# Twelve frequency groups: the second of two products replaced by ScalarE copies that exchange partition halves

## The chip, the cores and the metric

The kernel runs on one core of a Trainium2 chip. The metric is the time of one execution on the device in microseconds (us). The engines are PE (TensorE, matrix products into PSUM), DVE (VectorE), ACT (ScalarE), POOL (GpSimd, which works on SBUF only here) and SP (which issues DMAs); PEld is the loading of weights into PE.

## The reference

An input x of 2048 rows and 640 columns goes through two mixers, and a gate per row blends them:

```python
def _A_ref(x, wqkv, wo):       # 32 heads of 20, a window of 8 keys, every second row back
    qkv = (x @ wqkv).reshape(B, S, 3, H, Dh) ...
    logits = jnp.einsum("bhsd,bhswd->bhsw", q, kg) * scale
    attn = _softmax(where(mask, logits, -1e9))
    return einsum("bhsw,bhswd->bhsd", attn, vg).reshape(B, S, D) @ wo

def _B_ref(x, w_r, w_i):
    X = jnp.fft.rfft2(x)
    return jnp.fft.irfft2(X * (w_r + 1j * w_i), s=(S, D))

g = _sigmoid((x * gate_w).sum(-1, keepdims=True))
return g * a + (1 - g) * b
```

## The kernel before

Rows are held as 128 partitions of 16 rows j. The work has these stages. **qkv**: products of x and wqkv, split into two halves of precision, for even rows (`xe`) and odd rows (`xo`), written to a buffer in DRAM. **fold** and **cols**: the sums and differences of x that the spectrum needs, on DVE, and the first transform (tiles `fe`, `fx`, `z`). **attend**: per pair of head groups the products of q and k (`pr`, from a copy of q in a PSUM bank named `qbank`), their sums (`L`), maximum and exponential, the products with v on POOL (`pv`) and their sums on DVE (`o`); names such as `o4b6` carry the group, the half and the row. **freq**: the spectrum in 16 groups of frequencies, described below. **spatial** (tiles `oa`, `ob`, `ha`, `hb`, `h`, `y`): the transform back, odd rows first. **project**: the product with wo for even rows (`woa`, `wob`, `ya`), and at the very end for odd rows.

A frequency group g of `freq` works as follows. PE computes v and u out of zc, and DVE their sum and difference `ab`. PE multiplies `ab` with a table `tb`: `xa` and `xc` are the products of sum and difference, `xb` and `xd` the same with the table's columns in the turned order, which is the spectrum times the imaginary unit: the same numbers with their two halves of 64 partitions exchanged and one half negated. ACT copies `xa` and `xb` into `X`; POOL multiplies X by the weights `wp` and adds (`P`). DVE multiplies `xc` by a weight into `p` and `xd` by another in place, subtracts (`xd<-p,xd`), and adds to and subtracts from P (`s`). PE transforms `s` back (`g`), and ACT copies it into `zg`. The four products take their PSUM banks in turn out of two, BX = banks 3 and 4.

The order of all instructions is not written by hand. A planner records every operation with a duration and a delay (`Plan.cost`), sorts it by a list schedule forward and backward, then tries `AGAIN` random shifts of the priorities and keeps the best (`Plan.order`). Each engine runs its instructions in that order. Waits between engines come from a layer below, which sees the tiles that an instruction reads and writes. All instructions are issued from one line, L636 before and L638 after.

Of the kernel before, what the change touches and what calls it, by code (L numbers as in the profile page):

```python
# [27 lines left out]
BV, BU, BX, BG, BO = (0,), (1, 2), (3, 4), (5,), (6,)  # L28
# [127 lines left out]
class Plan:  # L156
# [84 lines left out]
    def cost(self, op, out, ins, k):  # L241
        n = max(int(np.prod(v.shape[1:])) for v in [out] + ins[:1])
        if op.name == "dma_start":
            op.busy, op.lat = {"SP": 0.45, "ACT": 0.45, "POOL": 1.0}[op.eng], LAND
            op.size = int(np.prod(out.shape)) * 4
            op.early = not hasattr(ins[0].tensor, "tag")
        elif op.eng == "PE":
            n = int(np.prod(out.shape[1:]))
            if op.name == "transpose":
                op.busy = 0.109  # L250
            elif ins[-1].dtype == F32R:
                op.busy = n / 2400 + 0.018
            else:
                op.busy = 4 * n / 2400 + 0.006
            op.lat = 0.25
        elif op.eng == "DVE":
            op.busy, op.lat = 0.075 + n / 960, 0.12
            two = sum(v.tensor.tag[:4] not in ("bank", "qban") for v in ins) == 2
            if op.name == "scalar_tensor_tensor":
                op.busy += 0.06  # L260
            elif op.name == "reciprocal":
                op.busy += n * 0.007
            elif two:
                op.two = True
        elif op.eng == "ACT":
            strided = any(len(v.ap) > 2 and v.ap[-1][0] > 1 for v in [out] + ins)
            op.busy, op.lat = 0.12 + n * (1.75e-3 if strided else 0.78e-3), 0.15
            if len(ins) > 1:
                op.busy += 0.1
        else:  # L270
            spread = any(v.ap[-1][0] == 0 for v in ins)
            op.busy, op.lat = 0.09 + n * (2e-3 if spread else 2.25e-3), 0.14
        if op.eng in ("DVE", "ACT", "POOL") and not op.size:
            op.busy *= PACE
# [192 lines left out]
                exec(*op.call)  # L467


TURNS, AGAIN, MOVE, SEED = 6, 60, 2.0, 2  # L470
DRAWS, SOONEST, LATER_BY = 3, 2.4, 0.6
ENGS = ("PE", "DVE", "ACT", "POOL", "SP")
RATE = 380e3
# [29 lines left out]
class Mixer:  # L503
# [64 lines left out]
    def work(self):  # L568
# [48 lines left out]
        p.chain = ""  # L617
        freq = [self.freq(g) for g in GORD]
        staged(freq, 4)
        p.chain = "even"  # L620
        for j in range(0, NJ, 2):
# [120 lines left out]
    def attend(self, par, h, step=4):  # L742
# [18 lines left out]
        for jj in range(0, 8, 2):  # L761
# [5 lines left out]
            else:  # L767
# [7 lines left out]
                in_=pr.rearrange("p j r (h d) -> p j r h d", d=HD),  # L775
                axis=AX.X,
                op=ALU.add,
# [3 lines left out]
        m = self.mr.next(f"m{nm}", 8, 4)  # L781
        V.tensor_reduce(out=m, in_=L, axis=AX.X, op=ALU.max)
        G.tensor_sub(L, L, m.unsqueeze(3).broadcast_to([128, 8, 4, 8]))
        A.activation(out=L, in_=L, func=AF.Exp, scale=SCALE)
        s = self.sr.next(f"s{nm}", 8, 4)
        V.tensor_reduce(out=s, in_=L, axis=AX.X, op=ALU.add)
        V.reciprocal(s, s)
        G.tensor_mul(L, L, s.unsqueeze(3).broadcast_to([128, 8, 4, 8]))
        yield
        for jj in range(0, 8, 2):  # L790
# [4 lines left out]
            for i in range(2):  # L795
# [4 lines left out]
                )  # L800
            V.tensor_reduce(out=o[:, jj % step : jj % step + 2], in_=pv, axis=AX.X, op=ALU.add)
            if jj % step == step - 2:
# [65 lines left out]
    def freq(self, g):  # L868

        p, ins = self.p, self.ins  # L870
        V, A, G, T, S = p.dve, p.act, p.pool, p.pe, p.sp
        zg, bt = self.zg, self.bt
        if g == 0:
            tb = self.one("tbfirst", 1280, tag="x7")
            S.dma_start(tb, ins["t_first"])
        else:
            if g % 3 == 1:
                self.mm = self.mdr.next(f"mm{g}", 3, 320)
                S.dma_start(self.mm, ins["t_mm"][(g - 1) // 3])
            tb = self.mm[:, (g - 1) % 3]  # L880
        wp = self.wpr.next(f"wp{g}", 4, 321)
        self.queue("wp").dma_start(wp, ins["ws"][g])

        zc = self.zcr.next(f"zc{g}", 6, NJ, 8)
        A.copy(zc[:, 0:3], zg[:, 0:3, :, 8 * g : 8 * g + 8])
        A.mul(zc[:, 3:6, :, 0:4], zg[:, 2:5, :, 8 * g + 4 : 8 * g + 8], -1.0)
        A.copy(zc[:, 3:6, :, 4:8], zg[:, 2:5, :, 8 * g : 8 * g + 4])

        def row(o, t, r, start, stop):
            T.matmul(o, zc[:, t].rearrange("p j c -> p (j c)"), r, start=start, stop=stop, skip_group_check=True)  # L890

        v = self.ps(BV, f"v{g}")[:, 0:321]
        row(v, 4, bt[:, 803:1124], True, False)
        row(v[:, 0:161], 3, bt[:, 642:803], False, False)
        row(v[:, 161:321], 5, bt[:, 1124:1284], False, True)
        vv = self.vsr.next(f"vs{g}", 321)
        A.copy(vv, v)
        u = self.ps(BU, f"u{g}")[:, 0:321]
        row(u, 1, bt[:, 161:482], True, False)
        row(u[:, 0:161], 0, bt[:, 0:161], False, False)  # L900
        row(u[:, 161:321], 2, bt[:, 482:642], False, True)

        ab = self.abr.next(f"ab{g}", 2, 321)
        V.tensor_add(ab[:, 0], u, vv)
        V.tensor_sub(ab[:, 1], u, vv)
        yield

        def col(nm, i, turned):

            o = self.ps(BX, f"{nm}{g}")[:, 0:321]  # L910
            if g == 0:
                c = 256 * i + 128 * turned
                T.matmul(o, tb[:, c : c + 128], ab[:, 0], start=True, stop=False)
                T.matmul(o, tb[:, 512 + c : 640 + c], ab[:, 1], start=False, stop=True)
            else:
                c = 0 if turned else 64
                T.matmul(o, tb[:, c : c + 128], ab[:, i], start=True, stop=True)
            return o

        X = self.Xr.next(f"X{g}", 2, 321)  # L920
        for i, nm in enumerate(("xa", "xb")):
            A.copy(X[:, i], col(nm, 0, i))
        P = self.Pr.next(f"P{g}", 2, 321)
        G.tensor_mul(P, X, wp[:, 0:2])
        G.tensor_add(P[:, 0], P[:, 0], P[:, 1])
        yield
        z, sz = col("xc", 1, 0), col("xd", 1, 1)
        t = self.p1r.next(f"p{g}", 321)
        V.tensor_mul(t, z, wp[:, 2])
        V.tensor_mul(sz, sz, wp[:, 3])  # L930
        V.tensor_sub(sz, t, sz)
        s = self.s12r.next(f"s{g}", 768)
        d0 = 321
        if g == 0:
            d0 = 449
            G.memset(s[:, 384:449], 0.0)
        V.tensor_add(s[:, 0:321], P[:, 0], sz)
        V.tensor_sub(s[:, d0 : d0 + 319], P[:, 0, 2:], sz[:, 2:])
        yield

        last = s[:, 640:768] if g == 0 else s[:, 512:640]
        chunks = [[(s[:, 0:128], 0)], [(s[:, 128:256], 0)], [(s[:, 256:384], 0)], [(s[:, 384:512], 1)], [(last, 1)]]
        if g == 0:
            chunks[2:4] = [[(s[:, 384:512], 1), (s[:, 256:321], 0)], [(s[:, 512:640], 1)]]
        for t0, n in ((0, 3), (3, 2)):
            o = self.ps(BG, f"g{g}_{t0}")
            for i in range(n):
                for w, back in chunks[t0 + i]:
                    m = tb[:, 1024 + 128 * back : 1152 + 128 * back] if g == 0 else tb[:, 192:320]
                    T.matmul(  # L950
                        o[0 : w.shape[1], i * 128 : i * 128 + 128],
                        w,
                        m,
                        start=(i == 0),
                        stop=(i == n - 1),
                        skip_group_check=True,
                    )
            A.copy(
                zg[:, t0 : t0 + n, :, 8 * g : 8 * g + 8],
                o[:, 0 : n * 128].rearrange("p (t j c) -> p t j c", t=n, c=8),  # L960
            )
# [166 lines left out]
POOL_PR = {u: (6,) for u in ((0, 3), (0, 4), (0, 5), (0, 7), (1, 0), (1, 1), (1, 3), (1, 4), (1, 5), (1, 7))}  # L1128


def build(tc, ins, out):
    Mixer(tc, ins, out).run()

# [43 lines left out]
```

## Time and profile before

| | us |
|---|---|
| median of 3 runs | 467.83 |
| lowest and highest | 467.37, 468.66 |
| span of the profiled execution | 465.3 |
| outside the span, median less span | 2.5 |

The page gives no time of the profiled execution beside its span, so the last row takes the median for it. The frequency stage lies from about 235 to 353 us, with attention beside it; spatial and the even projections follow to about 423, and the odd projections end the span. In the profile's rows a group is "line engine operation out<-in by names (numbers left out), shapes, count | busy us, mean ns | idle before us, and what ended it". A float32 product appears as two records, a product of the split type (fp32r) as one.

### The profile page before, as it was taken

To read this page: it belongs to the slowest core of one execution; us is meant where nothing else is said; L and a number is where in the kernel's file an instruction comes from. 1 tells how busy PE (TensorE), PEld (TensorE's weight loads), DVE (VectorE), ACT (ScalarE), POOL (GpSimd) and SP (SyncE) were. 2 spreads that over 40 slices of the span, in tenths; PEclk is the share of its full clock that TensorE was granted. 3 is DMA by queue.
4 is the path that set the end of the run, shared out by engine and by line. 5 is a ranking of instruction groups with operands and counts; after the bars stand their busy time and mean duration, and the time that the engine had idled before them with its cause. 6 is when DMAs were issued, how large, how long until landed. Compare 5 with 4: busy or idle time off the path is not lost.

```text
span 465.3 us, 7240 instructions
## 1 busy us (share of the span) xinstructions
PE 457.0 (98%) x2497; PEld 399.5 (86%) x2497; DVE 423.4 (91%) x555; ACT 205.2 (44%) x539; POOL 323.9 (70%) x264
## 2 busy tenths in 40 slices
PE   7999999999999999999999999999999999999997
PEld 4788888888889888899887788898888999988996
DVE  4699959999999999998999999999999997989784
ACT  5523346533335453257356465545444564333110
POOL 1003847999999879988698996767877997952300
PEclk9999999999999999999999999999999999999999
DMA  8999998796877968959998466567543321447732
GB/s 310 403 376 308 393 381 314 230 299 197 242 216 252 322 187 275 282 167 276 343 258 307 135 217 220 185 183 234 182 129 120 103 80 56 136 141 220 227 113 85
DMA packets 71700, 105.90 MB, mean 228 GB/s; under 512 B 20704, under 2 KB 50400, under 8 KB 71664
## 3 DMA queue, kind: packets, MB, share of 16 engines
q1 hardware_dynamic: 40624, 69.90, 46.0%
q10 hardware_dynamic: 30128, 31.55, 20.9%
q0 software_dynamic: 912, 4.00, 2.1%
q8 instruction: 19, 0.31, 0.3%
q14 instruction: 17, 0.14, 0.1%
HBM read 72.59 MB, written 32.84 MB: 227 GB/s over the span
## 4 chain that ended last, share of the span: by engine, by line
PE 82%; DVE 10%; DMA 4%; issue 2%; ACT 0%; ACTq 0%; DVEq 0%
PE qkv L636 43%; PE wob L636 6%; PE woa L636 6%; PE z L636 4%; PE ob L636 4%; PE oa L636 4%; PE u L636 2%; PE v L636 2%; PE hb L636 2%; PE g L636 2%; PE ha L636 2%; DVE xd L636 2%; DMA fx<-in_x 2%; PE oTp L636 2%; DVE s L636 1%
## 5 line engine op out<-in xcount | busy, mean ns | idle before, releaser
L636 PE MATMUL qkv<-w,xo 128*128 128x480 f32 (+1 forms) x480 | 110.7, 384 | 0.0
L636 PE MATMUL qkv<-w,xe 128*128 128x480 f32 (+1 forms) x465 | 104.1, 382 | 1.1 <-DVE xe L636 0.7
L636 PEld LDWEIGHTS qkv<-w,xe 128*128 128x128 f32 x465 | 87.3, 188 | 17.1 <-ACT xe L636 1.8
L636 PEld LDWEIGHTS qkv<-w,xo 128*128 128x128 f32 x480 | 89.8, 189 | 13.7
L636 ACT COPY ev<-qkv 128x480 f32<-128x480 f32 x64 | 35.4, 558 | 71.9 <-PE qkv L636 60.9
L636 PE MATMUL woa<-wo,oT 128*128 128x320 f32 x240 | 51.2, 317 | 0.1
L636 PE MATMUL wob<-wo,oT 128*128 128x320 f32 x240 | 50.4, 314 | 0.0
L636 PEld LDWEIGHTS wob<-wo,oT 128*128 128x128 f32 x240 | 39.0, 188 | 0.8 <-ACT ya L636 0.2
L636 PEld LDWEIGHTS woa<-wo,oT 128*128 128x128 f32 x240 | 39.0, 188 | 0.7 <-ACT oT L636 0.4
L636 POOL TENSOR_TENSOR w<-raw,w 128x480 fp32r<-128x480 f32 (+1 forms) x20 | 28.6, 1442 | 11.1 <-ACT w L636 11.1
L636 POOL TENSOR_TENSOR P<-X,wp 128x642 f32<-128x642 f32 x16 | 25.0, 1562 | 15.4 <-ACT X L636 15.4
L636 POOL DMA_DIRECT2D fd<-fx x6 | 4.3, 717 | 37.5 <-DMA raw<-in_wqkv 31.3
L636 POOL TENSOR_TENSOR yi<-yi,y 128x640 f32<-128x640 f32 x8 | 12.4, 1558 | 20.5 <-DMA yi<-ad 14.9
L636 ACT CAST oT<-oTp 128x384 fp32r<-128x384 f32 (+1 forms) x32 | 13.1, 427 | 29.9 <-PE oTp L636 25.2
L636 PEld LDWEIGHTS g<-mm,s 128*128 128x128 f32 x150 | 21.5, 191 | 3.6 <-ACT zg L636 0.2
L636 PE MATMUL g<-mm,s 128*128 128x128 f32 x150 | 22.7, 274 | 0.0
L636 PE MATMUL oa<-gt,zg 128*128 128x161 f32 (+1 forms) x96 | 22.1, 344 | 0.0
L636 PE MATMUL u<-bt,zc 128*128 128x321 f32 (+2 forms) x96 | 22.1, 344 | 0.0
L636 PE MATMUL v<-bt,zc 128*128 128x321 f32 (+2 forms) x96 | 22.1, 344 | 0.0
L636 PE MATMUL ob<-gt,zg 128*128 128x161 f32 (+1 forms) x96 | 21.0, 344 | 0.0
L636 ACT CAST w<-raw 128x480 fp32r<-128x480 f32 (+1 forms) x30 | 17.4, 594 | 7.4 <-DMA raw<-in_wqkv 2.2
L636 PEld LDWEIGHTS v<-bt,zc 128*128 128x128 f32 x96 | 16.3, 190 | 4.0 <-ACT vs L636 0.2
(301 smaller groups left out, 1118.7 us busy)
## 6 DMA issues: line engine op xcount, KB each, us to landing
qkvd<-ev ACTq DMA_DIRECT2D x32, 480.0 KB, 4.8
wp<-in_ws SPq DMA_DIRECT2D x16, 642.0 KB, 4.4
raw<-in_wqkv SPq DMA_DIRECT2D x25, 240.0 KB, 5.8
fx<-in_x SPq DMA_DIRECT2D x8, 641.0 KB, 9.0
ot<-od SPq DMA_DIRECT2D x16, 320.0 KB, 3.4
fd<-fx POOLq DMA_DIRECT2D x6, 640.0 KB, 8.5
f<-fd SPq DMA_DIRECT2D x6, 640.0 KB, 5.5
xt<-in_xT SPq DMA_DIRECT2D x8, 320.0 KB, 6.3
```

The costliest lines, as they stand in the source:

```text
L636: p.dve.memset(w, 0.0)
```

## The change

For the groups 4 to 15 the products `xb` and `xd` are gone. A helper `turn` makes the same values by two ACT operations over 64 partitions each: the lower half from the upper, negated, and the upper half from the lower. For X the source is `xa`, the target `X[:, 1]` in SBUF; for `xd` the source is `xc`, the target a PSUM bank taken from the same two. Such a group now takes three turns of the banks, not four. The planner gets 0.08 us more for an ACT operation with an operand that begins at partition 64 or above, and tries 100 shifts in place of 60. Groups 0 to 3 stay as they were.

```diff
@@ Plan.cost
             if len(ins) > 1:
                 op.busy += 0.1
+            if any(v.offset >= 64 * v.ap[0][0] for v in [out] + ins):
+                op.busy += 0.08
@@
-TURNS, AGAIN, MOVE, SEED = 6, 60, 2.0, 2
+TURNS, AGAIN, MOVE, SEED = 6, 100, 2.0, 2
@@ Mixer.freq
+        def turn(to, o):
+
+            A.mul(to[0:64], o[64:128], -1.0)
+            A.copy(to[64:128], o[0:64])
+
         X = self.Xr.next(f"X{g}", 2, 321)
-        for i, nm in enumerate(("xa", "xb")):
-            A.copy(X[:, i], col(nm, 0, i))
+        o = col("xa", 0, 0)
+        A.copy(X[:, 0], o)
+        if g in TURN:
+            turn(X[:, 1], o)
+        else:
+            A.copy(X[:, 1], col("xb", 0, 1))
...
-        z, sz = col("xc", 1, 0), col("xd", 1, 1)
+        z = col("xc", 1, 0)
+        if g in TURN:
+            sz = self.ps(BX, f"xd{g}")[:, 0:321]
+            turn(sz, z)
+        else:
+            sz = col("xd", 1, 1)
@@
+TURN = tuple(range(4, 16))
```

PE has 1979 products in the program in place of 2003, ACT 36 operations more; DVE, POOL and SP have the same instructions in another order. Three places of that order follow.

The first is DVE in group 8 of the frequency stage, before the change, from `ab` of group 9 on. What an instruction waits for stands in brackets, by engine or DMA queue.

```order
L636 TENSOR_TENSOR ab9_743<-u9_742,vs9_741 128x321 [waits PE_49]
L636 TENSOR_TENSOR ab9_743<-u9_742,vs9_741 128x321
L636 TENSOR_TENSOR p8_748<-xc8_746,wp8_722 128x321 [waits DMAHW5_49,PE_49]
L636 TENSOR_TENSOR pr5a4_536<-kt5a_530,qbank_63 128x1280 [waits Activation_49]
L636 TENSOR_TENSOR xd8_747<-xd8_747,wp8_722 128x321 [waits PE_49]
L636 TENSOR_TENSOR xd8_747<-p8_748,xd8_747 128x321 [waits DVE_49]
L636 TENSOR_TENSOR s8_749<-P8_737,xd8_747 128x321 [waits DVE_49,Pool_49]
```

The same place of DVE after the change:

```order
L638 TENSOR_TENSOR oT2_856<-oTp3_858,oT2_856 128x256 [waits Activation_49]
L638 TENSOR_TENSOR p8_743<-xc8_741,wp8_718 128x321 [waits DMAHW1_49,Activation_49]
L638 TENSOR_TENSOR pr5a4_536<-kt5a_530,qbank_63 128x1280
L638 TENSOR_TENSOR xd8_742<-xd8_742,wp8_718 128x321 [waits Activation_49]
L638 TENSOR_TENSOR xd8_742<-p8_743,xd8_742 128x321 [waits DVE_49]
L638 TENSOR_TENSOR s8_744<-P8_732,xd8_742 128x321 [waits DVE_49,Pool_49]
```

DVE's product p and its multiplication of xd waited for PE, and now for ACT (Activation). ACT's side of it in the changed order:

```order
L638 ACTIVATE X8_730<-xa8_731 64x321 [waits PE_49,Pool_49]
L638 COPY zg_210<-g6_3_725 128x32x8 [waits PE_49]
L638 COPY X8_730<-xa8_731 64x321
L638 CAST oT2_856<-oTp3_858 128x256 [waits PE_49]
L638 COPY X8_730<-xa8_731 128x321
L638 ACTIVATE xd8_742<-xc8_741 64x321 [waits PE_49,Activation_49]
L638 COPY xd8_742<-xc8_741 64x321 [waits DVE_49]
L638 COPY zg_210<-g7_0_739 128x48x8 [waits PE_49]
```

The second half copy waits for DVE (its p), so in this group ACT and DVE alternate. So it is in groups 4, 6, 7, 8, 9, 10 and 12; in 5, 11, 13 and 15 both half copies stand ahead of p, and in 14 p stands ahead of both.

The second place is ACT near 52 to 63 us, in the first attention group, before the change, from the last cast of the weight block w2 on:

```order
L636 CAST w2_4_159<-raw2_4_158 128x480
L636 COPY ev1_6_148<-qkv1_6_147 128x6x80
L636 CAST w3_0_173<-raw3_0_172 128x480
L636 CAST w3_1_175<-raw3_1_174 128x480
L636 CAST w3_2_177<-raw3_2_176 128x480
L636 COPY qbank_63<-q0a_340 128x160
L636 COPY L0a_341<-low_80 1x8x2
L636 COPY ev1_6_148<-qkv1_7_149 128x6x80
L636 COPY qbank_63<-q0b_356 128x160
```

And after the change:

```order
L638 CAST w2_4_159<-raw2_4_158 128x480
L638 DMA qkvd_64<-ev1_4_145 128x6x160
L638 COPY qbank_63<-q0a_340 128x160
L638 CAST w3_0_173<-raw3_0_172 128x480
L638 COPY qbank_63<-q0b_356 128x160
L638 CAST w3_1_175<-raw3_1_174 128x480
L638 COPY L0a_341<-low_80 1x8x2
L638 CAST w3_2_177<-raw3_2_176 128x480
L638 COPY ev1_6_148<-qkv1_6_147 128x6x80
```

The copies into `qbank` of q0a and q0b (ACT) now stand two rows apart around the first of three casts of a weight block (`w3_0`, `w3_1`, `w3_2`), and ahead of the copies of `qkv1_6` and `qkv1_7`; before, they stood behind all three casts. DVE's third `pr0a` waits for both copies in either order.

The third place is DVE near 423 to 426 us, before the change, around the last even output `y14`:

```order
L636 SCALAR_TENSOR_TENSOR h14_1021<-ha14_1019,nng_75,h14_1021 128x160
L636 TENSOR_TENSOR oT1_1027<-oTp0_1028,oT1_1027 128x384
L636 SCALAR_TENSOR_TENSOR ha14_1019<-ha14_1019,ng_74,h14_1021 128x160
L636 TENSOR_TENSOR y1_1025<-ye1_1024 128x321
L636 TENSOR_TENSOR y1_1025<-ye1_1024 128x319
L636 TENSOR_TENSOR ye3_1030<-ho1_921 128x2x161
L636 SCALAR_TENSOR_TENSOR ha14_1019<-ha14_1019,ng_74,h14_1021 128x161
L636 TENSOR_TENSOR y14_1023<-ha14_1019,h14_1021 128x321
L636 TENSOR_TENSOR y14_1023<-ha14_1019,h14_1021 128x319
L636 TENSOR_TENSOR ye3_1030<-ho1_921 128x160
L636 TENSOR_TENSOR oT3_1033<-oTp3_1035,oT3_1033 128x256
```

And after the change:

```order
L638 SCALAR_TENSOR_TENSOR ha14_1007<-ha14_1007,ng_74,h14_1009 128x160
L638 SCALAR_TENSOR_TENSOR ha14_1007<-ha14_1007,ng_74,h14_1009 128x161
L638 TENSOR_TENSOR oT1_1015<-oTp0_1016,oT1_1015 128x384
L638 TENSOR_TENSOR y14_1011<-ha14_1007,h14_1009 128x321
L638 TENSOR_TENSOR y14_1011<-ha14_1007,h14_1009 128x319
L638 TENSOR_TENSOR oT3_1021<-oTp3_1023,oT3_1021 128x256
L638 TENSOR_TENSOR oT3_1021<-oTp0_1022,oT3_1021 128x384
L638 TENSOR_REDUCE o4b6_596<-pv4b6_597 128x160
L638 TENSOR_TENSOR y1_1013<-ye1_1012 128x321
L638 TENSOR_TENSOR y1_1013<-ye1_1012 128x319
L638 TENSOR_TENSOR ye3_1018<-ho1_909 128x2x161
```

The two `y1`, a `ye3` and the last attention reduction `o4b6` stood ahead of `y14` (o4b6 22 rows ahead) and now follow it. Nothing else crosses y14.

## The prediction

> **What bounds the kernel now.** I read the page's table of engines first, then the stretches, then the chain of waits.
>
> ```profile
> span 465.3 us, 7240 instructions
> PE 457.0 (98%) x2497; PEld 399.5 (86%) x2497; DVE 423.4 (91%) x555; ACT 205.2 (44%) x539; POOL 323.9 (70%) x264
> PEclk9999999999999999999999999999999999999999
> ```
> TensorE (PE) is busy in 98% of the span at a full clock, VectorE (DVE) in 91%. The span stands to the median of the runs, 467.83, as 465.3 + 2.5 us around it; the page gives no other time of that execution, so I add every change of the span to the median. About 0.3% (1.4 us) is what a measurement here can tell from no change.
>
> The next table cuts the span at the start of the frequency stage (235), its end (353), the end of the even rows (423). Columns: length, busy time and instructions of PE, PEld, DVE, ACT and POOL, then clock and DMA.
>
> ```profile
> 20.00:235.00 215.00, 214.84 (x1060) 187.22 (x1061) 204.42 (x202) 93.75 (x246) 167.05 (x129) 1.00 0.85 282
> 235.00:353.00 118.00, 116.76 (x670) 99.06 (x669) 114.94 (x178) 62.30 (x179) 94.06 (x82) 1.00 0.64 205
> 353.00:423.00 70.00, 69.52 (x440) 63.29 (x439) 64.61 (x92) 34.19 (x85) 56.18 (x42) 1.00 0.34 101
> 423.00:465.30 42.30, 38.85 (x272) 38.27 (x270) 30.39 (x72) 5.10 (x13) 4.66 (x3) 1.00 0.50 163
> ```
> The reader is to see two engines at their limit in the changed stage: PE 116.76 of 118, DVE 114.94 of 118. DVE's idle time by stretch is 10.6, 3.1, 5.4 and 11.9 us. The chain of waits, asked for the end of the frequency stage, shows which of the two paces it:
>
> ```profile
> 341.02 0.32 DVE m5b L636
> 341.34 0.40 DVE ab L636
> 341.74 0.40 DVE p L636
> 342.14 0.40 DVE ab L636
> 342.54 0.41 DVE xd L636
> ...
> 343.58 0.90 DVE s L636 x2
> ...
> 344.52 0.81 PE xb L636 x2
> ```
> From about 302 to 344 nearly every piece is DVE; PE is on the chain before and after it. So a PE saving in this stage is worth only what DVE can follow.
>
> **What is removed.** 24 products, xb and xd of groups 4 to 15. A float32 product is two records in the trace:
>
> ```profile
> 241.53 0.54 PE xa L636 x2
> 242.07 0.54 PE xb L636 x2
> ```
> 24 x 0.54 = 13.0 us of PE, all in the frequency stage, on an engine without cover. That is the floor: no gain beyond 13.0, unless the new order also shortens PE's own waits.
>
> **What is added.** Each of 12 groups loses one ACT copy (X from xb) and gains four half-partition operations (two into X, two into xd). Nearest rows by number of elements:
>
> ```profile
> L636 ACT COPY X<-xb 128x321 f32<-128x321 f32 x16 | 6.8, 428 | 8.8 <-PE xb L636 8.6
> L636 ACT ACTIVATE ya<-woa,g 128x320 f32<-128x320 f32 x5 | 2.6, 527 | 10.2 <-PE woa L636 10.2
> ```
> No row moves data between partition halves. I take 0.43 each, the copy of equal width per partition out of the same memory; 0.53, the scaled one, is the upper end; the lower end is 0.24, which is what a 64-element copy takes in the row quoted with the early wait below. 12 x (4 x 0.43 - 0.43) = 15.5 us more ACT. In this stage ACT is busy 62.3 of 118, so 77.8 of about 110 after: covered in total. If the cover goes, the price is that of the last rival.
>
> **What is moved: a hand-off in each group.** Before, DVE's product p reads xc and its multiplication reads xd, both straight from PE. After, the order has DVE wait for ACT at both. In groups 4, 6, 7, 8, 9, 10 and 12 p stands between the two half copies: first copy, p, second copy, xd, each with a wait on the one before; in 5, 11, 13 and 15 p waits for both copies; in 14 p is ahead of both. The second copy holds ACT's queue until DVE has done p, and behind it stand copies of zg (for PE's next products) and of X (for POOL). In six of the seven alternating groups DVE has other work between p and xd (ab, or a reduction or product of 1.4 us) that covers the copy. A hop between the two engines:
>
> ```profile
> 393.50 0.53 ACT L636 ACTIVATE h<-hb,ng 128x322 f32<-128x322 f32 x1 [0.94 <-PE hb L636]
> 394.07 0.39 DVE L636 SCALAR_TENSOR_TENSOR h<-ha,ng,h 128x161 f32<-128x161 f32 x1 [1.68 <-ACT h L636]
> ```
> ACT ends at 394.03, DVE starts at 394.07: 0.04 us. Bounds per group on DVE: 0, if PE runs ahead and xc is copied before DVE comes to it; 2 x 0.43 + 2 x 0.04 = 0.94, if nothing covers. I take 0.25, near the low end because PE has 13 us less to do: 12 x 0.25 = +3.0 (0 to +11.3).
>
> The Trainium skill, page PSUM — Partial Sum Buffer, section PSUM bank collisions raise a hardware error, says that two engines may not touch the same bank and 32-partition quadrant at once, two reads included, and that such pairs are kept apart by a dependency; so p and the copies of xc cannot overlap. If they could, this term would be about 0 and the forecast 457.1 instead of 460.1. No row of this trace has ACT and DVE reading one bank together, but the waits in the changed order agree.
>
> **DVE's own work.** Its instructions are the same 555, in another order. Ahead of the last even output (y14, the pair at 425.31) the new order has four fewer: the reduction o4b6 (1.48, as its like at 414.69) and, for the odd rows, two y (0.88) and one ye (0.41).
>
> ```profile
> 414.69 1.48 DVE L636 TENSOR_REDUCE o4b<-pv4b 128x160 f32<-128x1280 f32 x1
> 423.56 0.88 DVE L636 TENSOR_TENSOR y<-ye 128x321 f32<-128x321 f32 x2
> 424.48 0.49 DVE L636 TENSOR_TENSOR ye<-ho 128x322 f32<-128x322 f32 x1
> 425.31 0.89 DVE L636 TENSOR_TENSOR y<-ha,h 128x321 f32<-128x321 f32 x2
> ```
> 1.48 + 0.88 + 0.41 = -2.8 (ye counted to the next start). They follow in the last stretch, where PE's odd products set the pace and DVE idles 11.9; cost there nothing, and 2.8 if that cover went.
>
> **DVE's waits.** Three kinds change. First an early one:
>
> ```profile
> 57.22 1.49 DVE L636 TENSOR_REDUCE L0a<-pr0a 128x64 f32<-128x1280 f32 x1
> 62.91 1.49 DVE L636 TENSOR_TENSOR pr0a<-kt0a,qbank 128x1280 f32<-128x1280 f32 x1 [4.20 <-ACT qbank L636]
> ```
> What ACT did meanwhile, and one issue of a store on POOL's queue:
>
> ```profile
> 58.76 1.26 ACT L636 CAST w<-raw 128x480 fp32r<-128x480 f32 x2
> 61.31 0.60 ACT L636 CAST w<-raw 128x480 fp32r<-128x480 f32 x1 [1.29 <-DMA raw<-in_wqkv]
> 62.59 0.28 ACT L636 COPY qbank<-q0b 128x160 f32<-128x160 f32 x1
> 63.14 0.24 ACT L636 COPY L0a<-low 1x64 f32<-1x64 f32 x1 [0.26 <-ACT qbank L636]
> ...
> 54.67 0.71 POOL L636 DMA_DIRECT2D fd<-fx x1
> ```
> DVE lost 4.20 us because the copies into qbank stood in ACT's queue behind three casts, the third of which waited for its DMA until 61.31. The new order puts the copy from q0a ahead of all three and that from q0b behind the first only. That cast started at 58.76, so the second copy ends near 58.76 + 0.63 + 0.28 = 59.7, against DVE ready at 58.7. POOL's queue now has one more store ahead of the split of w2, which frees the buffer for that cast's data; an issue takes 0.71. I take -3.0 (0 to -4.2).
>
> Second, the frequency stage idles 3.1 now, of which these are the only waits of 0.2 or more:
>
> ```profile
> DVE xd L636 <- PE xd L636: 0.5, 1, 0.5
> DVE ab L636 <- ACT vs L636: 0.2, 1, 0.2
> ```
> With PE ahead I take -2.5 (0 to -3.1), beside the +3.0 above. Third, the 5.4 us from 353 to 423:
>
> ```profile
> DVE h L636 <- ACT h L636: 3.9, 5, 1.7
> DVE s4b L636 <- ACT L4b L636: 0.7, 1, 0.7
> ```
> ACT's h waits there for PE's hb (the 0.94 above); PE arrives earlier now, while DVE's reductions do not: -2.4 (0 to -5.4).
>
> **The sum** along DVE to the last even output: -2.8 - 3.0 + 3.0 - 2.5 - 2.4 = -7.7. Behind it both orders have the same PE work (eight odd rows), so the end moves as much: span 457.6, time 467.83 - 7.7 = 460.1. PE then idles 13.0 - 7.7 = 5.3 more than now. POOL (94.06 of 118) and SP's loads of wp and mm, unchanged in number, come sooner by the same few microseconds and have that room.
>
> **The rivals.**
> PE keeps pace to the floor: all DVE waits above go (-2.8 - 4.2 - 3.1 - 5.4 = -15.5), no hand-off shows, and PE's 13.0 binds: 454.8. For it: PE is 98% busy. Against: DVE would have to drop from 11.9 + 5.4 + 3.1 us of idle time behind 235 to 20.4 - 13.0 = 7.4, with ACT newly in its path.
>
> DVE already paces all, and its waits only change their places: what is left is the 2.8 of moved work: 465.0. For it: the DVE chain above. The Trainium skill, page Perfetto Trace Analysis, section Identifying the Most-Contended Engine, judges TensorE by its weight loads, not by matmul time, which would make DVE (91%) and not PE (86%) the engine to relieve; this trace agrees only in part, since PE's products follow one another without gaps (241.53 + 0.54 = 242.07).
>
> No change: the early wait stays, the late ones stay, and each hand-off costs half of its upper bound: -2.8 - 2.5 + 12 x 0.47 = +0.3, 468.1.
>
> Slower: the alternation of ACT and DVE is fully exposed, with copies at the scaled price: 12 x (2 x 0.53 + 2 x 0.04) = 13.7 in place of the 3.0: -7.7 - 3.0 + 13.7 = +3.0, 470.8. It decides from 12.1 us of hand-offs, 1.0 a group. For it: ACT's queue is in order and now waits for DVE in seven groups; against: DVE has work between.
>
> **How the numbers follow.** Forecast (457 to 464) 0.53; floor 0.12; 465.0 0.10; no change 0.10; slower 0.15. Faster by over 0.3%: 0.53 + 0.12 + 0.10 = 0.75. The time is that of the likeliest, 460.1. The range reaches from the floor, 454.8, to the no-change case's end, 468.5, leaving out slower and a few hundredths below.
>
> **What would show it.** PE's 321-wide records down by 48, 13.0 us; half copies near 430 ns; the 4.20 wait under 1.5; the waits for ACT h under 3; DVE waits on ACT in the frequency stage at about 3 in all; the chain there on DVE. The prediction is wrong if DVE waits more than 6 us for xd's copies, if a half copy takes over 0.6, or if POOL's sums P arrive late because X is copied late.

## The result and the profile after

The changed kernel took 463.31 us (461.7 to 464.1, 4 runs) beside 467.6 (467.21 to 468.66, 4 runs) for the kernel before: a ratio of 0.9898, with a 95% interval of 0.9876 to 0.992. That is 4.3 us faster where 7.7 were forecast. The profiled execution took 463.47 us, its span 461.7. Its page begins:

```profile
span 461.7 us, 7202 instructions
...
PE 449.5 (97%) x2449; PEld 393.3 (85%) x2449; DVE 422.1 (91%) x555; ACT 219.4 (48%) x575; POOL 319.5 (69%) x264
...
PEclk9999999999999999999999999999999999998999
```
PE has 48 records less. ACT has 14.2 us more, where 15.5 were reckoned. One digit of the granted clock is an 8, in the slice from 415.5 to 427.1; before there was none. The stretches, with the columns as before (length, busy PE, PEld, DVE, ACT, POOL, clock, DMA):

```profile
0.00:20.00 20.00, 17.35 (x57) 11.64 (x57) 8.87 (x14) 8.95 (x16) 1.99 (x9) 1.00 0.92 342
20.00:235.00 215.00, 213.67 (x1055) 186.63 (x1056) 205.85 (x203) 93.77 (x245) 165.25 (x131) 1.00 0.86 281
235.00:353.00 118.00, 115.62 (x674) 98.25 (x674) 113.00 (x178) 80.29 (x224) 91.64 (x80) 1.00 0.66 211
353.00:423.00 70.00, 67.55 (x420) 61.82 (x419) 67.84 (x99) 31.56 (x78) 57.46 (x43) 0.98 0.38 115
423.00:461.70 38.70, 35.29 (x248) 34.94 (x247) 26.54 (x64) 4.82 (x12) 3.13 (x2) 1.00 0.45 146
```
In 235 to 353 ACT has risen from 62.30 to 80.29, since its copies come there. The new thing is the fourth row: PE idles 2.45 us between 353 and 423, where it idled 0.48, at a clock of 0.98. The half copies, grouped by form:

```profile
L638 ACT ACTIVATE X<-xa 64x321 f32<-64x321 f32 x12 | 5.2, 436 | 3.4 <-PE xa L638 3.1
L638 ACT COPY X<-xa 64x321 f32<-64x321 f32 x12 | 5.0, 419 | 0.2
L638 ACT ACTIVATE xd<-xc 64x321 f32<-64x321 f32 x12 | 4.9, 411 | 2.4 <-PE xc L638 1.5 <-DVE p L638 0.6
L638 ACT COPY xd<-xc 64x321 f32<-64x321 f32 x12 | 4.8, 399 | 3.2 <-DVE p L638 3.0
```
A copy of 64 partitions takes about as long as one of 128 (428 ns before), though all of these cross from one half to the other. DVE's waits up to 425:

```profile
DVE p L638 <- ACT xd L638: 2.9, 6, 0.6
...
DVE pr0b L638 <- ACT qbank L638: 2.0, 1, 2.0
...
DVE h L638 <- PE ha L638: 0.8, 1, 0.8
...
DVE pr0a L638 <- ACT qbank L638: 0.7, 1, 0.7
```
The early wait of 4.20 is 0.7, the waits for ACT's h (3.9) are gone, and the hand-off at p stands there with 2.9. The chain of waits runs through that hand-off twice between 300 and 346, here the first time, and through PE for longer than before:

```profile
306.63 0.56 PE xc L638 x2
307.22 0.04 issue
307.27 0.42 ACT xd L638
307.69 0.02 issue
307.71 0.49 DVE p L638
...
310.06 0.42 DVE xd L638
...
311.10 0.50 DVE s L638
311.60 0.14 issue
311.74 0.91 PE g L638 x6
312.65 2.20 PE woa L638 x15
```
Last, PE around the first odd row's transposes (oTp) and its projection (woa, wob), asked as a timeline:

```profile
414.49 0.78 PE L638 MATMUL oTp<-ident,ot 128*128 128x128 f32 x5
415.83 0.56 PE L638 MATMUL wob<-wo,oT 128*128 128x320 f32 x2 [0.57 <-ACT oT L638]
416.22 0.46 PE L638 MATMUL woa<-wo,oT 128*128 128x320 f32 x2
418.44 0.90 PE L638 MATMUL oTp<-ident,ot 128*128 128x128 f32 x3 [1.76 <-DVE oT L638]
418.99 1.15 PE L638 MATMUL woa<-wo,oT 128*128 128x320 f32 x3
```
And DVE's queue there:

```profile
414.35 1.48 DVE L638 TENSOR_REDUCE o4b<-pv4b 128x160 f32<-128x1280 f32 x1
415.74 0.48 DVE L638 TENSOR_TENSOR y<-ha,h 128x321 f32<-128x321 f32 x1
...
417.84 0.55 DVE L638 TENSOR_TENSOR oT<-oTp,oT 128x384 fp32r<-128x384 f32 x1
```
PE needs a PSUM bank back that DVE's oT (417.84) has to read first, and that stands behind a reduction and six even-row operations. PE waits, and then runs at half clock:

```profile
418.00:421.50 3.50, 3.06 (x12) 3.06 (x13) 3.12 (x6) 0.48 (x1) 2.76 (x3) 0.51 0.76 233
```
The Trainium skill, page TensorE: Matmul & The Clock Gate, section What's actually happening, gives a free-running window of about 3.4 us, and half rate after one idle window. The length agrees (0.51 over 3.5 us). The condition is looser here: PE worked from 415.83 to 416.68, between gaps of 0.57 and 1.76.

The fall of the clock does not come in every execution. Of the four, two had a mean granted clock of 0.996 (463.47 and 464.10 us) and two of 1.000 (463.15 and 461.70).

**Where PE's 13.0 us went.** In each of the two traces I added up by how much PE's records start later than is usual behind a record of the same shape. Usual is the lower quartile of the distances from start to start, 0.27 us for a record 321 wide. This finds delays that a busy share hides:

```
lost by late starts, us    before   after   more
0 to 30 (start, DMAs)         7.3     9.4    2.2
30 to 235                     1.6     1.6   -0.1
235 to 353 (frequency)        3.8     7.6    3.8
353 to 413                    1.0     1.1    0.1
413 to 430 (first odd row)    1.7     5.1    3.4
430 to the end                0.5     1.0    0.4
```
The last column adds up to 9.8. 13.0 less 9.8 is 3.2; the span fell by 3.6.

### The profile page after: what moved, and what is told of

It is laid out like the page before. It is cut to its first block, busy times and chain, and to the rows that moved or that the text cites. A ratio compares the mean times of both kernels' runs of the same rounds, so it can differ in the third digit from the quotient of the medians.

```text
span 461.7 us, 7202 instructions
## 1 busy us (share of the span) xinstructions
PE 449.5 (97%) x2449; PEld 393.3 (85%) x2449; DVE 422.1 (91%) x555; ACT 219.4 (48%) x575; POOL 319.5 (69%) x264
## 4 chain that ended last, share of the span: by engine, by line
PE 83%; DVE 9%; DMA 4%; ACT 2%; issue 2%; SPq 0%; ACTq 0%; DVEq 0%
PE qkv L638 43%; PE woa L638 7%; PE wob L638 6%; PE z L638 4%; PE oa L638 3%; PE ob L638 3%; PE g L638 3%; PE u L638 2%; PE v L638 2%; PE oTp L638 2%; PE xc L638 2%; DMA raw<-in_wqkv 2%; DMA st<-in_xT 1%; PE hb L638 1%; PE ha L638 1%
## 5 line engine op out<-in xcount | busy, mean ns | idle before, releaser
L638 POOL TENSOR_TENSOR w<-raw,w 128x480 fp32r<-128x480 f32 (+1 forms) x20 | 25.3, 1278 | 8.0 <-ACT w L638 5.3
L638 PEld LDWEIGHTS g<-mm,s 128*128 128x128 f32 x150 | 22.5, 190 | 6.4 <-ACT zg L638 1.7
L638 PE MATMUL g<-mm,s 128*128 128x128 f32 x150 | 24.9, 278 | 1.4 <-DVE s L638 0.7
L638 PE MATMUL u<-bt,zc 128*128 128x321 f32 (+2 forms) x96 | 23.3, 344 | 0.0
L638 PE MATMUL ob<-gt,zg 128*128 128x161 f32 (+1 forms) x96 | 23.1, 344 | 0.0
L638 POOL TENSOR_TENSOR yi<-yi,y 128x640 f32<-128x640 f32 x8 | 12.6, 1569 | 14.2 <-DMA yi<-ad 11.4
L638 DVE TENSOR_TENSOR oT<-oTp,oT 128x384 fp32r<-128x384 f32 (+1 forms) x32 | 15.2, 482 | 3.7 <-ACT oT L638 3.7
```

The source lines that it names most:

```text
L638: p.dve.memset(w, 0.0)
```

## The experiments

Unless said otherwise, an order is "frozen": the planner's order of the changed kernel is kept, and the edit is made where it is issued. "Planned anew" means that the planner ran on the edited work. Each is set beside runs of the kernel before on the same chip.

**1. The tail: one DVE operation moved.** `e1_tail`:

```diff
 order = self.order()
+op = <second DVE piece of oT1>; a = order.index(<last o4b4 on DVE>)
+held = <DVE operations between them: y, h, h, y, ha, ha of even rows>
+<op stands right behind o4b4, held behind op>
```

> The changed kernel, its order frozen, but for one move on DVE: the second piece of oT for the first odd row (128x384, which stood behind y, h, h, y, ha, ha and ended at 418.39) stands right behind the reduction o4b that ends at 415.83. Theory (the lead of 7.0 us at the last even output shrinks to 3.6 at the end because PE stood still for 1.76 us before oTp at 418.44 and then ran 3.4 us at half clock): PE's wait for DVE's oT falls under 0.8 us, no slice behind 415 shows a granted clock under 0.9, and the time falls by 2 to 3.5 us to 459.8 to 461.3. If the stall alone counts and the clock drops all the same: about -1.5, 461.8. Rival (the odd rows are bound by something else, for instance their loads of ot or DVE's outputs): within 1 us of 463.3.

461.16 us, ratio 0.9854 (0.9834 to 0.9874). PE's wait for DVE's oT is 0.2 where it was 1.8, and the clock holds:

```profile
418.00:421.50 3.50, 3.50 (x26) 3.49 (x27) 3.36 (x10) 0.48 (x1) 3.50 (x3) 1.00 0.62 182
```
So the tail theory holds, with 2.2 us by the medians. About 1.6 of them are left where the clock did not fall: the three executions with a mean clock of 1.000 took 460.27 to 461.20, the changed kernel's two 461.70 and 463.15. (Its page has one 8 among the digits of the clock, which comes from the start, between 20 and 30 us.) The next table has, for nine of the traces, how much earlier than in the kernel before (in us) the first and the last product of the odd rows came:

```
                         first odd product   last odd product
changed kernel                  -6.3              -3.6
e4_after_60                     -5.9              -3.8
f3_no_handoff                   -7.0              -4.2
f4_less_dve                     -7.5              -3.5
e1_tail    (move made)          -4.3              -4.5
g1         (move made)          -3.4              -3.5
g2         (move made)          -3.4              -3.6
g4         (move made)          -7.1              -7.2
f1_x_only  (order of its own)   -5.1              -4.9
```
In the first four rows, without the move, 2.1 to 4.0 us of the lead are lost from the first odd row on; with the move nothing. f2 and g3 below, with orders of their own, lose 0.4 at most. (In the profiled execution of e1 the start alone was 1.1 us later than in that of the changed kernel.)

**2. PE's work put back.** `e2_pe_back`, frozen:

```diff
     exec(*op.call)
+    if op.eng == "PE" and op.of.split("_")[0] in <xa, xc of groups 4 to 15>:
+        exec(*op.call)
```

> The changed kernel, its order frozen, but each of the 24 products xa and xc of groups 4 to 15 is issued twice in a row (the second start writes the same values over the first), so PE does again 24 x 0.54 = 13.0 us of work while all copies, hand-offs and the order stay. Theory (the gain in the frequency stage is PE's saving, as far as DVE can follow): the time goes back to 466 to 471. Rival (the gain is the other order that the planner found, and PE's saving is lost behind DVE): at most +1.5 on the changed kernel, 463.3 to 464.8.

475.16 us, ratio 1.0153 (1.0119 to 1.0188): 11.9 above the changed kernel, for 13.0 us of PE work. Both forecasts were too low, the rival by far. A part of it is the clock: at a mean clock of 1.000 two executions took 472.2 and 472.5, about 9.9 above those of the changed kernel. PE's listed waits ahead of the first odd row add up to 2.2 us, against 2.0 in the changed kernel. That speaks for PE's own work, and against readers that got xa and xc 0.54 us later. Under this order PE's work counts for three quarters or more of its length. And with as many products as before, the new order and its copies are 7.6 us slower than the kernel before: by the medians the exchange costs 7.6, and saves 11.9.

**3 and 4. The planner's number.** `e3_before_100` and `e4_after_60`:

```diff
-TURNS, AGAIN, MOVE, SEED = 6, 60, 2.0, 2      # before, e3
+TURNS, AGAIN, MOVE, SEED = 6, 100, 2.0, 2
-TURNS, AGAIN, MOVE, SEED = 6, 100, 2.0, 2     # changed kernel, e4
+TURNS, AGAIN, MOVE, SEED = 6, 60, 2.0, 2
```

> The kernel before (24 products as they were, no half copies), with only the planner's second number at 100 instead of 60. Theory (the number is worth little by itself, and the gain hangs on the exchange): 466.2 to 469.0, no change. Rival (the longer search found the better order, the early copy into qbank above all): 462 to 465, and the wait of pr0a for qbank under 1.5 us here too.

> The changed kernel with the planner's second number at 60, as before. Theory (the exchange carries the gain): 462 to 465.5, 2 to 5 us under the kernel before. Rival (the search carries it): 466.5 to 468.5, no change.

469.05 (ratio 1.0036, 1.0021 to 1.0051), at the upper edge of its range, and 463.45 (0.9911, 0.9892 to 0.993). The search does not carry the gain. In these two cases a new plan of the same work moved the end by 0.1 and 1.5 us, so differences under 1.5 between kernels planned anew are not read below.

**5 and 6. Each half alone**, planned anew:

```diff
         A.copy(X[:, 0], o)
-        if g in TURN:          # f2: xb stays a product
+        if False:
...
         z = col("xc", 1, 0)
-        if g in TURN:          # f1: xd stays a product
+        if False:
```

> Only xb of groups 4 to 15 is replaced by half copies (into X); xd stays a product. 12 x 0.54 = 6.5 us of PE go, 12 ACT copies become 24 half copies, and DVE's p gets no hand-off with ACT. Planned anew, which moved the time by 0 to 1.5 us in the two runs with the planner's number. Theory PE (the saved PE time counts, less what is lost on the way): about half the gain, 464 to 466.5. Theory hand-off (what is lost of the 13 us is lost to the alternation of ACT and DVE at p and xd): without it all of the 6.5 shows, 460 to 462, under the changed kernel.

> Only xd of groups 4 to 15 is replaced (half copies of xc into the bank of xd); xb stays a product. 6.5 us of PE go, 24 half copies are added, and the hand-offs between ACT and DVE at p and xd are all there. Theory PE: about half the gain, 464 to 466.5, like the X half. Theory hand-off: they cost 2.9 on DVE and 3.7 on ACT and eat the saving, 466.5 to 468.5.

463.32 (0.9892, 0.9864 to 0.992) and 466.24 (0.9983, 0.9962 to 1.0004). X alone brings 4.2, more than half and less than all of its 6.5, and so lies between the two forecasts; xd alone 1.3, not told from no change, and at the border of the two. The X half has no hand-off with DVE, and its own order keeps the lead in the tail. X and xd together came to no more than X alone; only with the tail's move (461.16) is there a lead of 2.2 over it.

**7. No hand-off**, frozen; ACT's copies read wp, not xc:

```diff
-A.mul(xd[0:64], xc[64:128], -1.0); A.copy(xd[64:128], xc[0:64])
+A.mul(xd[0:64], wp[64:128, 2], -1.0); A.copy(xd[64:128], wp[0:64, 2])
```

> The changed kernel, its order frozen; the 24 half copies into xd read the table wp in SBUF instead of the product xc in PSUM, so that they and DVE's p no longer wait for each other (the second products' values are left out of the result by this). DVE's multiplication of xd still waits for the copies. Theory DVE (the prediction's: DVE paces the stage, and its 2.9 us of waits for the copies are on the path): 460 to 461. Theory PE (formed on the run with the products issued twice, where 13.0 us of PE cost 11.9: PE's queue sets the time, and DVE's waits lie beside it): 462 to 463.5.

461.04 us, ratio 0.9854 (0.9823 to 0.9884): 2.3 less than the changed kernel, at the edge of what theory DVE gave (460 to 461) and outside theory PE's. The two intervals just overlap, but at an equal clock the difference stands: 459.39 and 460.31 beside 461.70 and 463.15 at 1.000, 460.91 and 461.17 beside 463.47 and 464.10 at 0.996. No wait between p and xd's copies is left in the trace (the copies no longer wait for PE's xc either), and the copies themselves are no cheaper (434 and 427 ns, where they took 411 and 399). So the hand-offs cost something, though 8 says that DVE has time.

**8. Less DVE work**, frozen; `f4_less_dve`:

```diff
-V.tensor_mul(sz, sz, wp[:, 3])     # groups 4 to 15
```

> The changed kernel, its order frozen; DVE's multiplication of xd by wp is left out in groups 4 to 15 (its factor is missing from the result): 12 x 0.41 = 4.9 us of DVE go. Theory DVE (DVE paces the frequency stage): 458.4 to 460. Theory PE: 461.8 to 463.5, within 1.5 us of the changed kernel.

463.01 us, ratio 0.9886 (0.9859 to 0.9914): nothing for 4.9 us of DVE. But the trace has a lead of 7.5 at the first odd product and 3.5 at the end, so the tail could have hidden it (five of the six executions had a mean clock of 0.996 or less); hence 12.

**9 and 10. The place of p**, frozen, with the tail's move; the seven alternating groups alone:

```diff
-copy, p, copy, xd      # order of issue
+copy, copy, p, xd      # g1
+p, copy, copy, xd      # g2
```

> The kernel with the tail's move (461.16), its order frozen; in the seven groups where DVE's p stood between ACT's two half copies into xd, both copies now stand ahead of p, so ACT never waits for DVE there (3.7 us of ACT's waits go) and p waits 0.4 longer for ACT in each. If ACT's queue carries the price of the hand-offs (its copies of zg and X, for which PE waits, stand behind the second half copy): 459 to 460.3. If DVE's waits carry it: 461.2 to 463. If the price is in neither and the 2.3 us that went with the reads from wp came from ACT no longer waiting for the product xc: 460.7 to 461.7, no change.

> The same seven groups the other way: p ahead of both half copies, so DVE's p no longer waits for ACT (most of the 2.9 us go) and ACT waits for DVE before its first copy. If ACT's queue carries the price: 461.2 to 463. If DVE's waits carry it: 459 to 460.3. If neither: 460.7 to 461.7.

463.72 (0.9916, 0.99 to 0.9932) and 461.76 (0.9882, 0.9865 to 0.9898), beside 461.16 (0.9834 to 0.9874) without the edit. DVE's waits in 230 to 350, of g1 and then of g2:

```profile
DVE p L653 <- ACT xd L653: 5.2, 8, 1.0
```

```profile
DVE p L653 <- ACT xd L653: 1.7, 4, 0.6
```
And 235 to 345, of e1 and then of g1:

```profile
235.00:345.00 110.00, 107.93 (x623) 91.01 (x622) 104.54 (x167) 75.75 (x214) 85.90 (x76) 1.00 0.69 219
```

```profile
235.00:345.00 110.00, 105.56 (x608) 88.41 (x608) 102.35 (x164) 74.66 (x208) 83.42 (x74) 1.00 0.66 214
```
In g1 p waits 2.3 us longer than in e1 (2.9), PE is busy 2.4 less, and the end is 2.6 later, though ACT's waits for p fell from 3.7 to 0.8. 463.72 lies above all three forecasts, nearest to that of DVE's waits. So ACT's waits for p do not carry the price by themselves. In g2 p waits 1.2 less and ACT waits 6.5 for p (3.7 in e1); the time is not told from e1's. 461.76 is what was forecast for the case that ACT's queue carries the price (and 0.06 above the case of neither), not the 459 to 460.3 of DVE's waits. The two runs fit together if a delay of p counts, since it goes on through xd and s to PE's product g, and if in g2 ACT's longer waits took back what p gained; that is argued and not shown. Taking waits from p by another order on the same bank gained nothing measurable; taking the shared bank away (7) gained 2.3 by the medians.

**11. X in three more groups**, planned anew, xd a product everywhere:

```diff
-TURN = tuple(range(4, 16))
+TURN = tuple(range(1, 16))
```

> Only X is turned by half copies, now in groups 1 to 15 (15 products less, 8.1 us of PE, against 6.5 with groups 4 to 15, which took 463.32); xd stays a product everywhere. Planned anew. Theory PE: three products more are worth up to 1.6 us: 461.5 to 463.3. Rival (re-planning moves the end by more than that): anywhere from 461 to 465, and over 463.3 the three groups are worth nothing.

464.69 (0.9933, 0.992 to 0.9946), 1.4 above groups 4 to 15, which is within what a new plan can do. Three products fewer did not pay; whether the plan or the three groups are at fault is not separated.

**12. Less DVE work with the tail's move**, frozen:

```diff
+<the move of 1>
-V.tensor_mul(sz, sz, wp[:, 3])     # groups 4 to 15
```

> The kernel with the tail's move, its order frozen, and DVE's multiplication of xd by wp left out in groups 4 to 15 (its factor is missing from the result): 4.9 us less DVE where the stall at the first odd row no longer swallows a lead. Theory PE: 460 to 461.2. Theory DVE (what the run without the tail's move could hide, since its lead of 7.5 us at the first odd product shrank to 3.5): 456.5 to 458.5.

460.28 us, ratio 0.9841 (0.9826 to 0.9857), beside 0.9854 (0.9834 to 0.9874): 0.9 by the medians for 4.9 us of DVE, not told from nothing (1.2 among the executions with a mean clock of 1.000). Its row for 235 to 345:

```profile
235.00:345.00 110.00, 107.58 (x630) 91.51 (x628) 101.60 (x159) 76.71 (x215) 85.77 (x76) 1.00 0.68 218
```
DVE is idle 2.9 us longer than in e1, and PE is as busy. DVE's amount of work does not set the pace: of what was taken away about a quarter or less came through, by these numbers.

Of the kernels that compute the whole result, e1 (461.16) is the fastest: 2.2 us below the changed kernel and 6.4 below the one before.

## Why the prediction was right and wrong

**Right.** The sign; 48 records less; half copies (399 to 436 ns against 430 taken); the early wait (-3.5 against -3.0); the hand-offs at p (2.9 against 3.0); the four operations moved behind y14 (-2.8). DVE's later waits fell by more (last s to y14: 5.53 to 1.78, so -3.8 against -2.4). The waits at p are there (2.9 us), and none is listed when the copies read elsewhere (experiment 7). With that the Trainium skill's rule on two engines at one PSUM bank agrees (page PSUM — Partial Sum Buffer, section PSUM bank collisions raise a hardware error).

**The step that failed** is "Behind it both orders have the same PE work (eight odd rows), so the end moves as much". Up to y14 the total was nearly right: its end moved from 426.2 to 419.2, so -7.0 against -7.7. Behind y14 the same work is done, but not at the same pace: the lead shrank to 3.6, because PE ran ahead of what DVE's queue released and stood still, and its clock fell after that. The order that I quoted to show four operations behind y14 was not followed to PE's next need. The run with one DVE operation moved keeps the lead; by medians this is 2.2 us of the 3.4.

**A term mis-sized.** For the frequency stage I had DVE's idle time at +0.5 (hand-offs +3.0, old waits -2.5); it went from 2.9 to 5.0, +2.1 (between the first ab and the last s). DVE's operations took 1.2 us less in all up to y14, which I had at nothing. Ahead of the stage DVE's idle time fell by 1.3 and not by 3.0: the early wait fell by 3.5, but DVE's other idle time there rose by 2.2. So -2.8 - 1.3 + 2.1 - 3.8 - 1.2 makes the measured -7.0, and that the total came within 0.7 is partly luck: misses of +1.7, +1.6, -1.4 and -1.2 cancelled.

**The path was the wrong one.** "A PE saving in this stage is worth only what DVE can follow" does not hold: 13.0 us of PE put back cost 11.9 (9.9 at an equal clock), and 4.9 us of DVE taken away gave 0.3 and 0.9. The sum along DVE could be made at all because the two engines are tied to one another: with PE's work put back DVE's idle time up to the last s was 10.3 us above that of e1, whose start was as late (3.7 and 3.3 us behind the kernel before). The better ledger is PE's: 13.0, less 2.2 at the start, 3.8 in the frequency stage, 3.4 at the first odd row. The early wait that I put at -3.0 went, but the trace lists no wait of PE between 30 and 235 in either kernel, so nothing shows that this came through to the end; and PE lost 2.2 more at the start. By the rule that I had weighed from the Trainium skill, page Perfetto Trace Analysis, section Identifying the Most-Contended Engine (judge TensorE by weight loads: 86%, so DVE with 91% first), DVE would have been chosen, whose work counted for less here.

**The rivals.** The floor of 454.8 was missed because PE's products started later than they could; DVE's amount of work explains little of it. "DVE already paces all" (465.0) is out by experiments 2 and 12. "No change" (468.1) is out by the time, and the early wait on which it stood went. The slower case did not come, but a longer hold on p does cost: with p behind both copies in the seven groups, 2.6 us are lost. "The chain there on DVE" was half right: from 312 on PE's products stand on it for long stretches.

**Open.** Why PE starts later. Its 60th record of a qkv product ended 0.9 to 3.7 us later than in the one profile of before in all 13 traces, and 1.0 to 3.7 later in the eight that share the changed kernel's order there; so some of it varies between executions of one order, and I cannot say how much belongs to the order. Nothing was tried on it. What of the 3.8 us in the frequency stage is hand-offs is known only as far as experiment 7 goes. Nor was it tried to halve p by partitions, so that it follows each half copy.

## What to carry to other kernels

When two engines are both near full, ask each of them in turn: put its work back, or take some away, with the order frozen. A sum along one engine up to a point is not a sum to the end: follow what each moved operation releases, also behind the point where the work is the same again. A saving on a full engine that buys a hand-off in its place is best split into the parts with and without the hand-off; here the part without had nearly all of the gain.

## What the hardware showed

A copy out of PSUM by ACT costs about the same for 64 partitions as for 128 (419 and 427 ns for 321 elements into SBUF, 399 from PSUM to PSUM), so an exchange of halves is paid as two full copies.

PE's clock fell to half for 3.4 us (0.51 over 418 to 421.5) after two gaps of 0.57 and 1.76 us with 0.85 us of products between them; with the second gap taken away (e1) it did not. It also fell there in e4, after gaps of 0.70, 0.57 and 1.11, but not in e2, after 0.57 and 1.12. At the start, it fell in the five traces in which PE waited 1.86 to 2.48 us near 20 us (e1, e2, f3, g2, g3), for 3.4 us each time, and in none of the other nine, with waits up to 1.72; yet a wait of 1.96 at 214 us in f2 left it at 1.00. So the clock can halve after gaps well under 3.4 us, and the length of one gap does not decide alone.
